# Moving four sub-key score products and two weight steps into the last projection, with a branch hint, in an attention and PEER block

## The chip, the cores and the metric

The kernel runs on one core of a Trainium2 chip. A core has a matmul engine (TensorE, PE in the profile, its weight loads shown apart as PEld), a vector engine (VectorE, DVE), an engine for activations and copies (ScalarE, ACT), a general one (GpSimd, POOL), and an engine that mainly issues transfers (SyncE, SP). They run their own instruction streams and meet at semaphores. The metric is the device time of one execution in microseconds; lower is better. The kernel before takes 1779.33 us, the median of three runs (1779.2 to 1783.94).

## The reference, cut to what matters

One sequence of N = 2048 rows of D = 448 features goes through two blocks, both with a layer norm in front and a residual sum behind. The first is attention with 16 heads of 28 features. The second is PEER: each row picks, per head, 8 of 4096 experts by two lists of 64 sub-keys, and sums their outputs.

```python
q  = jnp.einsum("nd,dhc->nhc", xf, w_q)            # 16 heads, 2 x 256
s1 = jnp.einsum("nhd,ed->nhe", q[..., :dk], k1)    # 64 sub-key scores
s2 = jnp.einsum("nhd,ed->nhe", q[..., dk:], k2)    # 64 sub-key scores
# the 8 best of s1, of s2, and of their 64 sums, per head
g   = softmax(top_s)                               # over the 8 chosen experts
act = gelu(einsum("nd,nhkd->nhk", xf, u[top_e]))
out = einsum("nhk,nhk,nhkd->nd", g, act, v[top_e])
```

All is float32. The kernel writes a product as a high part times a high part plus two corrections, so that a product over 448 features is 11 matmuls (`products`).

## The kernel before, in words

The rows are worked on in four blocks of 512 (`b` = 0 to 3), each of four tiles of 128 (`j` = 0 to 3). The kernel has these stages.

1. `qkv` (up to about 158 us): layer norm, queries, keys and values for all rows, stored to device memory. It also computes a bound on the attention scores and writes a flag for whether it is exceeded; then the last values are made, each copied by ACT and stored to `v_d` by a transfer from ACT's queue (lines 355 and 356).
2. The branch on the flag (`values_load` on line 422, `tc.If` on line 423). It is taken by PE, DVE and SP. The body, which fixes up queries for large scores, isn't executed with these inputs. On the path around it SyncE steps through eight semaphores that the body would have raised.
3. Attention (about 158 to 940 us) for 16 units of (block, four heads). Woven into it are the folding of the sub-keys into the query weights (`Fold`; results in `wp_d`, four tensors of four heads each), the split of the expert weights, and, for blocks 0 to 2, the projection behind attention (`project`) and the search for the best sub-keys (`search`).
4. The last projection, of block 3, and then the sub-key scores of block 3 (about 940 to 1046 us), with the first block's expert weights beside them. This is where the change is.
5. The experts, block after block (about 1046 us to the end): scores of all rows with all 4096 experts, `gelu`, multiplication with the dense matrix `G` of weights, and the product with `v`.

In stage 4 three generators are woven.

- `project(3, 2, room)`, 12 steps and a closing one. Each of the four tiles passes six steps: transposes of the attention output on PE and a copy on ACT; the low parts on DVE (`lows`, lines 109 and 110); the product with `wo` on PE, 11 matmuls, and a copy on ACT (line 567); residual sum, statistics on DVE (lines 569, 603, 604), and the reciprocal root on POOL (lines 96 and 97); the norm on DVE (line 100), transposes on PE and a copy on ACT (line 577); the low parts on DVE. A tile starts two steps after the one before. The closing step has SyncE store the result to `x_d` (lines 589 and 590).
- `weights(0, G)`, called `w0`, 34 steps: one loads `st`, one makes the first factors, and then 32 steps of 16 rows. Each has DVE prepare the next 16 rows (line 835, a comparison `p`, and in turn line 814, `f`, or line 820, `fg`), PE do 32 small matmuls (line 850), and ACT copy the result to `G` (line 852). Two buffers hold `p` and two PSUM banks the results (name `A`).
- `kept_scores(3, pools)`, called `sc`, 20 steps. The 16 heads are four groups (`g`) of four. For each group one step has SyncE load the folded keys, a high and a low half of 1 MB each (line 627), and four steps, one for each tile, have PE do 11 matmuls (line 80, `M<-w,XHb` and `M<-w,XLb`) and ACT copy the result to a `ring` buffer (line 630). The groups use two buffers in turn: `sw0` for groups 0 and 2, `sw1` for groups 1 and 3. `sw1` lies where the projection's buffers were, so that it is opened after `r2.close()`.

`scores_of` and all of the projection's products and transposes take their PSUM result tile under the name `M`, of which there are two.

The order of the work on each engine is the order in which the program issues it (`manual_schedule`); nothing is reordered. It comes from `weave`: each generator has a number of steps and a stretch from `lo` to `hi`, its steps are put at equal distances in the stretch, and the earliest goes next. So a pair of numbers such as 0.05, 0.27 sets which step of one generator stands in front of which step of another, on every engine on which both issue something, SyncE's queue among them.

Between the two calls of `weave` in stage 4 three loads of expert weights are issued (`load_u`, line 934); after the second, the rows of block 0 are loaded (`load_X`).

Of the kernel before, what the change touches and what calls it, by code (L numbers as in the profile page):

```python
# [18 lines left out]
ET = mybir.EngineType  # L19
# [36 lines left out]
def block(ctx: ExitStack, tc: tile.TileContext, x, wqk, wv, wo, wq, k12, uT, v, cst, out):  # L56
# [57 lines left out]
    def weave(*gens):  # L114


        gens = [[lo + 0.5 * (hi - lo) / n, (hi - lo) / n, g] for g, n, lo, hi in gens]
        while gens:
            e = min(gens, key=lambda e: e[0])
            e[0] += e[1]  # L120
            if next(e[2], end) is end:
                gens.remove(e)
# [144 lines left out]
    with ExitStack() as c0:  # L267
# [81 lines left out]
        def values_of(b):  # L349
            for j in range(4):  # L350
                c = slice(128 * j, 128 * j + 128)
                pv = ps.tile([128, D], F32, name="pq", bufs=4)
                mm_all(pv, products(lambda t: XH[b][:, t, c], lambda t: XL[b][:, t, c],
                                    lambda t: wvh[:, t], lambda t: wvl[:, t]))
                nc.scalar.activation(vst[j][:, :, :DH], pv.rearrange("p (h d) -> p h d", h=H), AF.Copy)
                (nc.scalar if b > 1 else nc.sync).dma_start(v_d[:, b, :, j].rearrange("g p c -> p g c"),
                                                                    vst[j].rearrange("p (g h) d -> p g (h d)", g=4))
# [3 lines left out]
        def qkv():  # L361
            for b in range(NB):
                normed(b)
                if b < 2:
                    values_of(b)
            load_wqk(0)
            for g in range(4):
                w = wqks.pop(g)
                if g < 3:
                    load_wqk(g + 1)  # L370
                kmax = wk.tile([128, 8], F32, name="kmax")
                for b in range(NB):
                    pk = proj(w[0], b)
                    sq = wk.tile([128, 512], FR, name="sq")
                    nc.scalar.activation(sq, pk, AF.Square, scale=SCALE)
                    kf = wk.tile([128, 512], F32, name="f", tag="f")
                    nc.scalar.activation(kf, pk, AF.Identity, bias=ct[:, C_ONE:C_ONE + 1], scale=SCALE)
                    store(ks_d[g], b, kf)
                    pn = ps.tile([128, 512], F32, name="tr")
                    nc.tensor.matmul(pn, blk, sq, start=True, stop=True)  # L380
                    nc.vector.reduce_max(kmax[:, b:b + 1], pn, axis=AX.X)
                nc.vector.reduce_max(kmax[:, 4:5], kmax[:, :4], axis=AX.X)
                nc.vector.tensor_scalar(kmax[:, 4:5], kmax[:, 4:5], 1.002, None, op0=OP.mult)
                for b in range(NB):
                    pq = proj(w[1], b)
                    sq = wk.tile([128, 512], FR, name="sq")
                    nc.scalar.activation(sq, pq, AF.Square)
                    pn = ps.tile([128, 512], F32, name="tr")
                    nc.tensor.matmul(pn, blk, sq, start=True, stop=True)
                    bd = wk.tile([128, 512], F32, name="bd", bufs=1)  # L390
                    nc.scalar.activation(bd, pn, AF.Sqrt, scale=kmax[:, 4:5])
                    nc.vector.reduce_max(kmax[:, b:b + 1], pn, axis=AX.X)
                    qf = wk.tile([128, 512], F32, name="f", tag="f")
                    nc.vector.scalar_tensor_tensor(qf, bd, ct[:, C_NEG:C_NEG + 1], pq, op0=OP.mult, op1=OP.add)
                    store(qs_d[g], b, qf)
                nc.vector.reduce_max(kmax[:, 5:6], kmax[:, :4], axis=AX.X)
                nc.vector.tensor_tensor(big[:, g:g + 1], kmax[:, 4:5], kmax[:, 5:6], op=OP.mult)
                if g == 1:
                    load_q(0)
                    for n in range(2):  # L400
                        load_kv(n)
                if g == 2:
                    fold.append(Fold(raw_p))
            bigm = wk.tile([128, 1], F32, name="bigm")
            nc.vector.reduce_max(bigm, big, axis=AX.X)
            nc.vector.tensor_scalar(bigm, bigm, BOUND * BOUND, None, op0=OP.is_gt)
            warm = wk.tile([128, 1], F32, name="warm")
            nc.scalar.activation(warm, bigm, AF.Exp)
            pf = ps.tile([1, 128], F32, name="tr")
            nc.tensor.transpose(pf, bigm, ident)  # L410
            bm = wk.tile([1, 1], F32, name="bm")
            nc.vector.reduce_max(bm, pf, axis=AX.X)
            nc.vector.tensor_copy(flag, bm)
            for b in range(2, NB):
                values_of(b)

        qkv()

    att = ExitStack()
    P = {0: att.enter_context(tc.tile_pool(name="pm", bufs=1, space=PSUM, reuse_waits="tile"))}  # L420

    isbig = nc.values_load(flag[0:1, 0:1], engines=(ET.PE, ET.DVE, ET.SP), min_val=0, max_val=1)
    with tc.If(isbig != 0):  # L423
        with ExitStack() as c1:
            gp = c1.enter_context(tc.tile_pool(name="lpg", bufs=1))
            pg = c1.enter_context(tc.tile_pool(name="psg", bufs=1, space=PSUM))
            kS = gp.tile([128, N], FR, name="kSg")
            qS = gp.tile([128, N], FR, name="qSg")
            mx = gp.tile([128, NT], F32, name="mx")
            old = gp.tile([NT, 2, 128], F32, name="old")  # L430
            new = gp.tile([NT, 2, 128], FR, name="new")
            for h in range(H):
                g, j = divmod(h, 4)
                r = slice(32 * j, 32 * j + 32)
                for i in range(4):
                    p = slice(32 * i, 32 * i + 32)
                    nc.sync.dma_start(kS[p].bitcast(F32), ks_d[g][K_ROWS[i], r])
                    nc.sync.dma_start(qS[p].bitcast(F32), qs_d[g][Q_ROWS[i], r])
                for i in range(2):
                    nc.sync.dma_start(old[:, i], qs_d[g][i, 32 * j + 28].rearrange("(a b) -> a b", a=NT))  # L440
                for t in range(NT):
                    S = pg.tile([128, N], F32, name="Sg")
                    for c in range(4):
                        nc.tensor.matmul(S[:, 512 * c:512 * c + 512], qS[:, 128 * t:128 * t + 128],
                                         kS[:, 512 * c:512 * c + 512], start=True, stop=True)
                    nc.vector.reduce_max(mx[:, t:t + 1], S, axis=AX.X)
                mt = P[0].tile([NT, 128], F32, name="M")
                nc.tensor.transpose(mt, mx, ident)
                nc.vector.tensor_tensor(old[:, 0], old[:, 0], old[:, 1], op=OP.add)
                nc.vector.tensor_tensor(old[:, 0], old[:, 0], mt, op=OP.subtract)  # L450
                nc.vector.tensor_copy(new[:, 0], old[:, 0])
                nc.vector.tensor_tensor(new[:, 1], old[:, 0], new[:, 0].bitcast(F32), op=OP.subtract)
                for i in range(2):
                    nc.sync.dma_start(qs_d[g][i, 32 * j + 28].rearrange("(a b) -> a b", a=NT), new[:, i].bitcast(F32))
            halves(qs[0], qs_d[0], slice(0, 512))
# [399 lines left out]
    WEIGHTS = 34  # L855
# [81 lines left out]
    with tc.manual_schedule(engines={ET.PE, ET.DVE, ET.Activation, ET.Pool, ET.SP}):  # L937
        room = {"xt": [ring[4 * j + 2] for j in range(4)], "at": [ring[3], ring[7]]}
        pools = [tc.tile_pool(name="sw0", bufs=1, side="right", reuse_waits="tile")]
        with ExitStack() as c1:  # L940
            pools = [c1.enter_context(pools[0])]
            w0, sc = weights(0, G), kept_scores(3, pools)
            weave((project(3, 2, room), 12, 0, 0.25), (islice(w0, 1), 1, 0.01, 0.02), (islice(sc, 1), 1, 0.02, 0.03),
                  (islice(w0, 6), 6, 0.05, 0.27))
            r2.close()
            be = ctx.enter_context(tc.tile_pool(name="be", bufs=3, reuse_waits="tile"))
            for f in range(3):
                us[f] = load_u(f)
            c2 = c1.enter_context(ExitStack())
            pools.append(c2.enter_context(tc.tile_pool(name="sw1", bufs=1, reuse_waits="tile")))  # L950
            weave((w0, WEIGHTS - 7, 0.27, 1), (sc, 19, 0.27, 0.88))
            load_X(0)
    bv = ctx.enter_context(tc.tile_pool(name="bv", bufs=3, reuse_waits="tile"))
    gw = ctx.enter_context(tc.tile_pool(name="gw", bufs=2, side="right", reuse_waits="tile"))
# [128 lines left out]
```

## Time and profile before

| | |
|---|---|
| median of three runs | 1779.33 us |
| the profiled execution | 1780.06 us |
| its span, first to last instruction | 1778.3 us |
| mean granted clock of TensorE | 0.987 |
| busy time of PE, DVE, ACT, POOL | 1705.5, 1137.3, 885.1, 396.7 us |

The page of the profile gives the busy time of each engine and the span in 40 slices; with it go groups of instructions by line, the waits (who waited for whom), the chain of work that ended last, and the timeline, in which one row stands for one instruction or for several of a kind that follow each other (x11). Times in the timeline are the start in us from the span's start and the duration in us; in square brackets stands the idle time of that engine before it and what ended it. A table by stage gives the busy time of every engine within a stretch, the granted clock (1.00 is full speed) and the busy share of the DMA engines.

### The profile page before, as it was taken

Reading aid. Unit: us, or ns where it says so; the run is one execution under the profiler, and the core shown is the slowest. Engines: PE = TensorE matmul, PEld = TensorE weight load, DVE = VectorE, ACT = ScalarE, POOL = GpSimd, SP = SyncE. Lnnn points to the kernel's source line nnn. Section 1 sums busy time; section 2 is a strip of 40 time slices with the busy share of each in tenths; the row PEclk is TensorE's granted clock in tenths of the full one; section 3 lists DMA queues with packets and bytes.
Section 4 is the critical chain, followed back from the end, with each engine's and each line's share of the span. In section 5 each row is a group of like instructions: output and inputs, shape, how many; then the busy total and the mean of one; then the engine's idle time right before and its main releaser. Section 6 shows DMA issues by size and latency. Waiting matters only on the chain.

```text
span 1778.3 us, 36155 instructions
## 1 busy us (share of the span) xinstructions
PE 1705.5 (96%) x14113; PEld 1164.2 (65%) x14113; DVE 1137.3 (64%) x3584; ACT 885.1 (50%) x1176; POOL 396.7 (22%) x450
## 2 busy tenths in 40 slices
PE   7998999999999899989996999999999999999999
PEld 6775434445544445444544888888888888888888
DVE  6653665444777548764776789526994599249722
ACT  3544767876677666866683342223422243224321
POOL 3451455321176224662271000000000000000000
PEclk9998999999999999999998999999999999999999
DMA  8754788568865787478841545766466745674564
GB/s 255 251 185 141 257 268 260 181 219 301 312 210 170 285 311 257 154 257 336 298 140 63 199 153 190 230 220 208 129 196 194 238 143 178 195 254 153 166 199 156
DMA packets 141744, 378.41 MB, mean 213 GB/s; under 512 B 13568, under 2 KB 40960, under 8 KB 133376
## 3 DMA queue, kind: packets, MB, share of 16 engines
q1 hardware_dynamic: 137344, 373.94, 63.1%
q8 instruction: 114, 1.87, 0.4%
q10 hardware_dynamic: 4224, 2.10, 0.4%
q14 instruction: 62, 0.51, 0.1%
HBM read 298.39 MB, written 77.59 MB: 211 GB/s over the span
## 4 chain that ended last, share of the span: by engine, by line
PE 73%; DVE 9%; POOL 2%; issue 1%; ACT 1%; DMA 0%; DVEq 0%; POOLq 0%
PE M L80 20%; PE acc L1006 16%; PE A L501 10%; PE S L476 10%; PE A L80 8%; PE A L850 5%; DVE ti L676 1%; DVE pos L703 1%; DVE ti L675 1%; ACT P L479 1%; PE M L106 1%; DVE p L835 0%; POOL sel L727 0%; PE M L489 0%; DVE ts L702 0%
## 5 line engine op out<-in xcount | busy, mean ns | idle before, releaser
L479 ACT ACTIVATE P<-S 128x1024 f32<-128x1024 f32 x512 | 495.9, 1023 | 89.2 <-PE S L476 87.7
L1006 PE MATMUL acc<-v,w 128*128 128x448 f32 x1536 | 329.7, 369 | 0.4 <-DMA v<-vs 0.2
L1006 PEld LDWEIGHTS acc<-v,w 128*128 128x128 f32 x1536 | 288.0, 188 | 33.2 <-ACT w L980 1.0
L501 PE MATMUL A<-P,V 128*32 128x512 f32 x2048 | 279.4, 614 | 0.0
L476 PE MATMUL S<-qS,kS 32*128 32x512 f32 x3072 | 272.2, 433 | 5.7 <-SPq L423 5.0
L476 PEld LDWEIGHTS S<-qS,kS 32*128 32x128 f32 x3072 | 145.2, 186 | 160.6 <-issue 99.2
L980 ACT ACTIVATE w<-ring 128x512 fp32r<-128x512 f32 x128 | 80.6, 632 | 223.9 <-PE acc L1006 161.5
L835 DVE TENSOR_TENSOR p<-st,iota 128x2048 f16<-128x2048 f16 x128 | 154.6, 1220 | 37.2 <-PE A L850 35.5
L981 DVE TENSOR_TENSOR w<-ring,w 128x512 fp32r<-128x512 f32 x128 | 87.3, 688 | 120.2 <-ACT w L980 120.0
L80 PE MATMUL A<-XHb,u 128*128 128x512 f32 x568 | 143.6, 394 | 0.0
L80 PE MATMUL M<-w,XHb 128*128 128x512 f32 x512 | 137.9, 412 | 5.1 <-ACT st L84 5.0
L675 DVE MAX8 ti<-fresh 128x8 f32<-128x64 f32 x384 | 80.6, 210 | 85.1 <-ACT fresh L657 85.1
L979 DVE TENSOR_TENSOR ring<-ring,G 128x512 f32<-128x512 f32 x128 | 85.5, 684 | 74.1 <-ACT ring L966 70.5
L80 PEld LDWEIGHTS M<-w,XHb 128*128 128x128 f32 x512 | 92.4, 190 | 61.3 <-issue 31.1
L850 PEld LDWEIGHTS <-p 128*128 128x128 f16 x4096 | 108.7, 97 | 25.3 <-issue 14.5
L850 PE MATMUL A<-fg,p 128*128 128x32 f16 x4096 | 116.7, 177 | 5.0 <-DVE p L835 4.9
L80 PE MATMUL M<-XHb,u 128*128 128x512 f32 x456 | 120.3, 403 | 0.0
L80 PEld LDWEIGHTS A<-XHb,u 128*128 128x128 f32 x568 | 106.0, 188 | 21.6 <-ACT ring L966 0.7
L966 ACT ACTIVATE ring<-M 128x512 f32<-128x512 f32 x57 | 34.2, 600 | 142.6 <-PE M L80 142.6
L501 PEld LDWEIGHTS A<-P,V 128*32 128x32 f32 x2048 | 41.8, 108 | 93.9 <-issue 86.8
L966 ACT ACTIVATE ring<-A 128x512 f32<-128x512 f32 x71 | 42.3, 596 | 103.8 <-PE A L80 103.8
L852 ACT ACTIVATE G<-A 128x512 f32<-128x512 f32 x128 | 76.7, 599 | 34.3 <-PE A L850 34.0
(178 smaller groups left out, 2298.7 us busy)
## 6 DMA issues: line engine op xcount, KB each, us to landing
u<-us SPq DMA_DIRECT2D x128, 512.0 KB, 3.6
w<-wp SPq DMA_DIRECT2D x56, 1024.0 KB, 7.9
v<-vs SPq DMA_DIRECT2D x128, 448.0 KB, 3.3
kS<-ks SPq DMA_DIRECT2D x64, 512.0 KB, 4.8
V<-vd SPq DMA_DIRECT2D x64, 256.0 KB, 3.0
us<-hl SPq DMA_DIRECT2D x32, 512.0 KB, 6.3
wr<-in_wq_dram SPq DMA_DIRECT2D x32, 448.0 KB, 5.7
vs<-hl SPq DMA_DIRECT2D x32, 448.0 KB, 5.7
```

Of the source, the lines that this page charges most:

```text
L80: nc.tensor.matmul(ps, l, r, start=i == 0, stop=i == len(pairs) - 1)
L476: nc.tensor.matmul(S[j // 2][:, j % 2], kS[r, a, 128 * (k % 4):128 * (k % 4) + 128], qS[r, c], start=m == 0, stop=m == 2)
L479: nc.scalar.activation(Pt[:, 2 * i:2 * i + 2], S[i], AF.Exp)
L501: nc.tensor.matmul(O[n][32 * j:32 * j + 32], V[:, k % 4, j], Pt[:, j], start=k == 0, stop=k == NT - 1)
L675: nc.vector.max(t8[:, 4 * i + k], src[:, 64 * k:64 * k + 64])
L835: newest[0] = nc.vector.tensor_tensor(p1, pairs(0, s, TG, 128), ids(TG, 128), op=OP.is_equal).ins
L850: nc.tensor.matmul(ps[:, t], p1[:, a, :, u], f[:, s % TF // 2 + a, k, :, u], start=k == 0, stop=k == 1)
L852: nc.scalar.activation(G[:, :, s:s + TG], ps.rearrange("p t f -> p f t"), AF.Copy, scale=1.0 / GS)
L979: nc.vector.tensor_tensor(a, a, G[:, f], op=OP.mult)
L980: nc.scalar.activation(w[:, 0], a, AF.Copy)
L981: nc.vector.tensor_tensor(w[:, 1], a, w[:, 0].bitcast(F32), op=OP.subtract)
L1006: nc.tensor.matmul(acc[j][:, :D], l, r, start=f == 0 and k == 0, stop=f == 31 and k == 2)
```

## The change

It has two parts.

In the first weave of stage 4, `w0` makes 8 steps in place of 6, and `sc` makes four steps in the stretch from 0.125 to 0.29: the four products of group 0. In the second weave `w0` has two steps less, `sc` four less, and the stretches begin at 0.29 in place of 0.27; that of `sc` ends at 0.92 in place of 0.88. By the numbers the order after the change is as follows (P is a step of the projection, W one of the weights that multiplies, S a score, each counted from 0): P0 P1 P2 P3 W0 P4 P5 W1 P6 S0 W2 P7 W3 P8 S1 P9 W4 P10 S2 W5 P11 W6, the closing step, S3; then the three loads, W7, the load of group 1, W8, and the first score of group 1. Before it was P0 to P4, W0, P5, P6, W1, P7, P8, W2, P9, W3, P10, P11, W4, the closing step; then the three loads, W5, S0, W6, S1, W7, S2, W8, S3, W9, the load of group 1, W10, W11 and the first score of group 1.

At the branch, the `If` gets a label, and right after the flag is written a hint for that branch is put into the streams of PE, DVE and SP. A hint asks for the instructions at the branch's target to be fetched ahead. The values of blocks 2 and 3 are issued between the hint and the branch.

```diff
             nc.vector.reduce_max(bm, pf, axis=AX.X)
             nc.vector.tensor_copy(flag, bm)
+            tc.mark_branch_hint_location("bound", engines=(ET.PE, ET.DVE, ET.SP))
             for b in range(2, NB):
                 values_of(b)
...
     isbig = nc.values_load(flag[0:1, 0:1], engines=(ET.PE, ET.DVE, ET.SP), min_val=0, max_val=1)
-    with tc.If(isbig != 0):
+    with tc.If(isbig != 0, label="bound"):
...
             weave((project(3, 2, room), 12, 0, 0.25), (islice(w0, 1), 1, 0.01, 0.02), (islice(sc, 1), 1, 0.02, 0.03),
-                  (islice(w0, 6), 6, 0.05, 0.27))
+                  (islice(w0, 8), 8, 0.05, 0.27), (islice(sc, 4), 4, 0.125, 0.29))
             r2.close()
...
-            weave((w0, WEIGHTS - 7, 0.27, 1), (sc, 19, 0.27, 0.88))
+            weave((w0, WEIGHTS - 9, 0.29, 1), (sc, 15, 0.29, 0.92))
             load_X(0)
```

## The prediction

> **What bounds the kernel now.** I read the page first.
>
> ```profile
> span 1778.3 us, 36155 instructions
> ...
> PE 1705.5 (96%) x14113; PEld 1164.2 (65%) x14113; DVE 1137.3 (64%) x3584; ACT 885.1 (50%) x1176; POOL 396.7 (22%) x450
> ...
> PEclk9998999999999999999998999999999999999999
> ```
>
> TensorE is busy for 96% of the span, so a gain can only come from its idle time or from its clock. Two places matter: the branch on the flag near 158 us, and the last projection with what follows it, which begins near 942 us. The busy time by stage, cut at 975.1 us (the last projection is complete) and at 992.1 us, is:
>
> ```profile
> 942.00:975.10 33.10, 21.77 (x234) 18.58 (x234) 25.75 (x44) 9.81 (x17) 2.98 (x8) 0.84 0.16 50
> 975.10:992.10 17.00, 15.11 (x170) 12.27 (x171) 12.98 (x13) 4.18 (x7) 0.00 (x0) 0.80 0.84 325
> 992.10:1046.00 53.90, 51.62 (x876) 42.92 (x875) 42.54 (x41) 20.96 (x35) 0.00 (x0) 1.00 0.33 121
> ```
>
> The columns are length, then busy time of PE, PEld, DVE, ACT and POOL, granted clock, DMA share and GB/s. TensorE is idle for 33.10 - 21.77 = 11.3 us in the projection, 1.9 us in the next 17 us, and 2.3 us from there to 1046. The 11.3 us are what the new work is put into. Here is why they exist: the last row tile's own chain, in order of time.
>
> ```profile
> 962.19 0.29 DVE L110 TENSOR_TENSOR oh<-M,oh 64x128 fp32r<-64x128 f32 x1
> ...
> 963.44 1.06 PE L80 MATMUL M<-woh,oh 128*128 128x448 f32 x4
> ...
> 965.15 0.78 PE L80 MATMUL M<-woh,ol 128*128 128x448 f32 x3
> ...
> 965.96 0.54 ACT L567 ACTIVATE ring<-M 128x448 f32<-128x448 f32 x1 [1.73 <-PE M L80]
> ...
> 967.12 0.62 DVE L569 TENSOR_TENSOR ring<-ring,ring 128x448 f32<-128x448 f32 x1
> ...
> 968.44 0.18 DVE L604 BATCH_NORM_AGGREGATE mv<-st 128x2 f32<-128x6 f32 x1
> ...
> 968.97 0.55 POOL L97 TENSOR_TENSOR rstd<-rstd,lnpow 128x1 f32<-128x1 f32 x1
> ...
> 969.52 1.22 DVE L820 TENSOR_TENSOR fg<-f,st 128x2048 f16<-128x2048 f16 x1
> 970.67 1.22 DVE L835 TENSOR_TENSOR p<-st,iota 128x2048 f16<-128x2048 f16 x1
> 971.80 0.51 DVE L100 TENSOR_SCALAR xn<-ring,mv,rstd 128x448 f32<-128x448 f32 x1
> 972.46 1.09 PE L106 MATMUL M<-ct,xn 128*128 128x128 f32 x4 [4.23 <-DVE xn L100]
> ...
> 974.21 0.56 DVE L109 TENSOR_TENSOR XLb<-M,XHb 128x384 fp32r<-128x384 f32 x1 [1.90 <-ACT XHb L577]
> 974.78 0.29 DVE L110 TENSOR_TENSOR XHb<-M,XHb 64x128 fp32r<-64x128 f32 x1
> 975.11 0.69 DVE L814 TENSOR_TENSOR f<-st,iota 128x1024 f16<-128x1024 f16 x1
> 975.72 1.22 DVE L835 TENSOR_TENSOR p<-st,iota 128x2048 f16<-128x2048 f16 x1
> ```
>
> It alternates between five engines. A step of weights on VectorE stands inside it already: the two instructions from 969.52 to 971.80 take 2.28 us, and TensorE waits 4.23 us for what is queued behind them. The other kind of step, L814 and a compare, takes 0.61 us to its second start and so about 1.75 us in all. When the chain ends, at 975.07, SyncE proceeds:
>
> ```profile
> 975.14 0.32 SPq L589 DMA_DIRECT2D xd<-XHb  x1
> 975.51 0.42 SPq L590 DMA_DIRECT2D xd<-XLb  x1
> 976.02 3.51 SPq L934 DMA_DIRECT2D u<-us  x3
> 979.64 1.16 SPq L627 DMA_DIRECT2D w<-wp  x2
> ...
> DMA to landing us min/median/max: 10.0/10.8/11.7
> ```
>
> The last line is the time to landing of the two transfers of 979.64, which bring the folded keys of the second four heads (group 1). Their first half lands at 979.64 + 10.0 = 989.6, their second at about 980.3 + 11.7 = 992.0: 14.5 and 16.9 us after the projection is complete, for they queue behind two stores and three loads. TensorE then looks like this:
>
> ```profile
> 983.09 2.11 PE L80 MATMUL M<-w,XHb 128*128 128x512 f32 x8
> ...
> 985.75 0.97 PE L850 MATMUL A<-fg,p 128*128 128x32 f16 x32
> 986.57 2.12 PE L80 MATMUL M<-w,XHb 128*128 128x512 f32 x8
> ...
> 995.80 2.09 PE L80 MATMUL M<-w,XHb 128*128 128x512 f32 x8
> ```
>
> From start to start a score product (11 matmuls) costs 985.75 - 983.09 = 2.66 us and a step of weights (32) costs 986.57 - 985.75 = 0.82. Group 1 is first used at 995.80. So the four products of group 0 are what hides those transfers today, with 3.8 us to spare.
>
> **The change part by part.** *Scores into the projection.* Four products of group 0, 4 x 2.66 = 10.6 us of TensorE, move ahead, three of them into the idle time and the fourth just behind the projection. Two weight steps, 1.6 us of TensorE and 1.75 + 2.28 = 4.0 us of VectorE, move with them, and the step times in the weave now put a step of compares in front of each norm and in front of the last lows, where before only the last norm had one. ACT's four evacuations move too, each about the 0.54 us of the L567 row, hidden beside the products. No DMA moves in program order: the stores, the three loads and the keys of group 1 still come in that order, behind the projection's end.
>
> The chain again, with the new work in its place. The third tile's product before it ran at half clock:
>
> ```profile
> 957.90:961.30 3.40, 3.40 (x11) 2.76 (x9) 2.26 (x2) 0.60 (x1) 0.00 (x0) 0.50 0.06 16
> ```
>
> With a weight step ahead of it I take it at full clock, which gives back 3.4/2 = 1.7 us; a compare step of 1.75 more ahead of the last tile's first lows takes them again, and these end at 962.5 as before. The first score then occupies TensorE to 965.3, two weight steps to 966.9, the last tile's product (963.44 to 965.93 in the rows, 2.4) to 969.3, the copy to 969.9, sum and statistics (967.12 to 968.62, 1.5) to 971.4, POOL with its hand-over (0.9) to 972.3. A compare step of 1.75 goes first, then the norm: 974.6. The transposes and their copy take about 1.5, but VectorE has a 2.28 us step to 976.8 ahead of the lows of 0.86. The projection is complete at 977.7 in place of 975.07: **+2.6 us**. The second score fits into the old 4.23 us wait. Bounds of this term: 0 if idle time takes all, and +9.4 by the second rival below.
>
> *The wait that follows.* After 977.7 TensorE has the third score's tail, the weight steps, the fourth score and two steps more: about 6.2 us, to 984. Then comes the first product of group 1, whose keys land 14.5 and 16.9 us after 977.7, at 992.2 and 994.6. What is queued behind it on TensorE is every further step, and VectorE can only fill the two compare buffers. So about **8 us of idle time come back**, which takes most of what the projection gave. From 994.6: 7/11 of a product (1.7), 11 products (29.3), 23 steps at 0.81 (18.6), the 2.3 us of compare waits in the third stage row, and the clock:
>
> ```profile
> 158.10:166.00 7.90, 7.18 (x48) 3.21 (x52) 5.66 (x5) 3.88 (x4) 2.35 (x1) 0.50 0.60 185
> ...
> 977.80:981.80 4.00, 4.00 (x18) 3.18 (x15) 4.00 (x5) 0.60 (x1) 0.00 (x0) 0.50 1.00 315
> ```
>
> After two other pauses the granted clock was 0.50 for 4.0 and for 7.9 us of work; 2.4 us of that pass before the second half lands, which leaves (1.6 to 5.5)/2 = 0.8 to 2.7 us lost. I take 1.5. The end: 994.6 + 1.7 + 29.3 + 18.6 + 2.3 + 1.5 = 1048.0, against 1046.0: **+2.0 us**. From there on TensorE is the bound and the shift passes on.
>
> The Trainium skill, "TensorE: Matmul & The Clock Gate", section "What's actually happening", says that one idle window of about 3.4 us halves the clock and one busy window restores it; that speaks against a pause of 8 us, and the rows agree on the halving, while 7.9 us is longer than its one window. An estimate by that page would be 1.7 us in place of 1.5, and the end 0.2 us later.
>
> *The hint.* The branch on the flag, with the page's fetches between 155.2 and 156.6:
>
> ```profile
> L423 SPq EVENT_SEMAPHORE  x8: 17/17/17, 151.6 to 158.0; - x8
> ...
> L423 PEldq COMPARE_BRANCH  x1: 4368/4368/4368, 150.0 to 150.0; - x1
> ...
> 153.78 0.37 ACTq L356 DMA_DIRECT2D vd<-vst  x1
> ...
> 158.14 2.07 PE L476 MATMUL S<-qS,kS 32*128 32x512 f32 x14 [4.97 <-SPq L423]
> ...
> DMA to landing us min/median/max: 3.9/3.9/3.9
> ...
> q8 instruction: 1, 0.02, 5.1%
> ```
>
> TensorE's branch takes 4.37 us from 150.0, over at 154.4, yet its first matmul waits for SyncE's eight semaphore steps, which end at 158.0. They follow the landing of the last store of V, issued at 153.78 and landed 3.9 us later. So the branch's own time is hidden; what shows is that landing. I put 1.6 of its 3.9 us down to the one instruction fetch that falls into it,
>
> ```profile
> DMA to landing us min/median/max: 2.3/2.3/2.3
> ```
>
> which is what the store two before it took to land. If the hint moves that fetch forward, 1.6 us go. The other end is no gain, and a cost of three short instructions, which no row shows; by the 17 ns of a semaphore step they are nothing. I take **-1.6 us**, as the only fetch in that stretch is one that follows the branch.
>
> Sum: +2.0 - 1.6 = +0.4. The profiled execution took 1780.06 us, 0.73 above the median of 1779.33; by it the sum gives 1780.5, by the median 1779.7. I forecast **1780.0 us**: no change that a measurement of this kernel could tell, which is about 0.3%, or 5.3 us.
>
> **The rivals.** *The keys come in time.* If both halves of group 1 landed within 6.2 us of the projection's end, the 8 us wait would be gone: 983.9 + 12 x 2.66 + 23 x 0.81 + 2.3 = 1036.7, 9.3 us early, and with the hint 1768.4 us. For it speaks only that SyncE is idle in the projection; against it the rows of SyncE, in program order behind the stores. Half of the way there, and the hint, give 1774.
>
> *The last tile's chain pays for all of it (slower).* If only the 4.23 us wait covers the three scores (8.0), two steps (1.6) and the compares (4.0), the projection ends 13.6 - 4.2 = 9.4 us later, not 2.6. Everything behind shifts by 6.8 more: 1779.3 + 2.0 + 6.8 = 1788.1 us, and 1786.5 with the hint. It decides from a delay of 2.6 + 5.3 - 2.0 = 5.9 us on, or 7.5 with the hint's gain. For it: two PSUM buffers named M serve both the chain and the scores, so a score must wait for a buffer and then holds it.
>
> *The hint frees TensorE alone.* By this rival the branch is what holds TensorE, and it starts at about 154.5, 3.6 us early: 1777.7 us with the +2.0. Against it: the wait in the row of 158.14 names SyncE. The Trainium skill, "Runtime: NRT & Kernel Launch", section "Instruction fetch mechanics", states that a taken branch out of the loaded window stalls for a fetch; the 4368 ns branch agrees, but the rule alone does not say who waits. If the hint does nothing at all, the time is 1781.3.
>
> **How the numbers follow.** My forecast with the hint's two ends has 0.52, the keys in time, wholly or half, 0.18, the paying chain 0.22, TensorE freed by the hint 0.08. Faster by over 0.3% (below 1774.0) is the first rival, 0.18; slower (above 1784.7) is the second, 0.22; the rest, 0.60, is within. The range takes in half of the first rival and most of the second: 1771 to 1786.5. The likeliest case alone holds 1777 to 1783.
>
> **What would show it.** After the change: products L80 M<-w,XHb between 955 and 980; a wait of 7 to 9 us on TensorE, released by the DMA w<-wp, shortly after the three loads of u; a granted clock of 0.5 behind it; the projection's last L110 near 978; the last weight step near 1048. At the branch: the 4368 ns gone, and the first matmul of S near 156.5. I am wrong if there is no wait for w<-wp, if the projection ends after 981, or if compares on VectorE hold TensorE for more than 4 us behind the wait.

## The result, and the profile after

The changed kernel takes 1782.5 us, the median of fourteen runs (1777.78 to 1787.77); the kernel before, beside it, 1780.71 us (1778.56 to 1784.11). The ratio is 1.0008, with a 95% interval of 0.9998 to 1.0018: no change that can be measured. The profiled execution took 1777.78 us, the shortest of the fourteen and 4.7 us below their median, so single stretches are compared here, not its span.

The page of the changed kernel:

```profile
span 1776.0 us, 36157 instructions
PE 1700.6 (96%) x14113; PEld 1159.9 (65%) x14113; DVE 1134.5 (64%) x3584; ACT 884.8 (50%) x1176; POOL 397.4 (22%) x450
PEclk9999999999999999999999899999999999999999
```

TensorE is still the bound at 96%. Its last projection begins at 937.52 and is complete at 972.80; the first half of the second four heads' keys is there at 986.96; the experts begin at 1042.0. Busy time by stage, with the columns length, PE, PEld, DVE, ACT, POOL, granted clock, DMA share and GB/s:

```profile
155.90:157.80 1.90, 1.20 (x14) 0.74 (x14) 1.79 (x3) 0.90 (x1) 0.00 (x0) 0.99 0.28 100
157.80:161.20 3.40, 3.23 (x18) 1.03 (x18) 3.37 (x3) 2.92 (x4) 2.34 (x1) 0.50 0.73 232
...
937.52:972.80 35.28, 27.25 (x267) 22.49 (x267) 29.75 (x47) 10.98 (x19) 4.21 (x8) 0.95 0.15 46
972.80:986.96 14.16, 6.05 (x140) 5.25 (x140) 8.89 (x9) 3.59 (x6) 0.00 (x0) 0.77 0.95 370
986.96:990.64 3.68, 3.32 (x7) 2.22 (x8) 0.00 (x0) 0.00 (x0) 0.00 (x0) 0.50 1.01 427
990.64:1042.00 51.36, 49.59 (x867) 41.40 (x866) 42.84 (x43) 20.52 (x35) 0.00 (x0) 1.00 0.23 88
```

The idle time has moved. The projection takes 35.28 us, against 32.84 before (942.24, the first transposes, to 975.08), and TensorE idles for 35.28 - 27.25 = 8.0 us in it, 11.3 before. Behind it TensorE idled for 1.9 of 17 us before; now it is busy for only 6.05 of the first 14.16, while the DMA engines are 95% busy. Its own rows, in order of time, name the transfer:

```profile
974.43 2.11 PE L80 MATMUL M<-w,XHb 128*128 128x512 f32 x8
...
977.08 1.77 PE L851 MATMUL A<-fg,p 128*128 128x32 f16 x64
986.96 2.08 PE L80 MATMUL M<-w,XHb 128*128 128x512 f32 x4 [8.11 <-DMA w<-wp]
989.40 1.75 PE L80 MATMUL M<-w,XHb 128*128 128x512 f32 x4 [0.36 <-DMA w<-wp]
```

TensorE finishes the fourth product and two steps of weights, then waits 8.11 us, and 0.36 for the second half. SyncE's queue shows why the keys are late; it is the same order as before, and starts the moment the projection is complete (the x4 in the last row are the two halves of group 1 and, behind them, those of group 2):

```profile
972.86 0.32 SPq L590 DMA_DIRECT2D xd<-XHb  x1
973.23 0.42 SPq L591 DMA_DIRECT2D xd<-XLb  x1
973.75 3.54 SPq L935 DMA_DIRECT2D u<-us  x3
977.40 3.36 SPq L628 DMA_DIRECT2D w<-wp  x4
```

At the branch, first the instructions on its line (count, duration in ns, first and last start in us), then the timeline:

```profile
L424 SPq EVENT_SEMAPHORE  x8: 17/17/17, 151.1 to 155.8; - x8
L424 PEldq COMPARE_BRANCH  x1: 388/388/388, 149.5 to 149.5; - x1
```

```profile
153.24 0.37 ACTq L356 DMA_DIRECT2D vd<-vst  x1
...
155.90 1.20 PE L477 MATMUL S<-qS,kS 32*128 32x512 f32 x14 [3.27 <-SPq L424]
```

TensorE's branch takes 388 ns for 4368 before, and the first matmul of S starts 155.90 - 153.24 = 2.66 us after the last store of V is issued, for 4.36 before. TensorE is still released by SyncE.

A correction to the description of the change above: the hints do not run where they are written, behind the flag. In the trace's instruction records they stand at the head of the three engines' streams, at 0.72 to 0.80 us, 50 to 51 ns each.

### The profile page after: what moved, and what is told of

The parts are those of the page before. It is cut to its first block, busy times and chain, and to the rows that moved or that the text cites. A ratio compares the mean times of both kernels' runs of the same rounds, so it can differ in the third digit from the quotient of the medians.

```text
span 1776.0 us, 36157 instructions
## 1 busy us (share of the span) xinstructions
PE 1700.6 (96%) x14113; PEld 1159.9 (65%) x14113; DVE 1134.5 (64%) x3584; ACT 884.8 (50%) x1176; POOL 397.4 (22%) x450
## 4 chain that ended last, share of the span: by engine, by line
PE 72%; DVE 8%; DMA 2%; POOL 2%; issue 1%; ACT 1%; SPq 0%; DVEq 0%; POOLq 0%; ACTq 0%
PE M L80 20%; PE acc L1007 16%; PE A L502 10%; PE S L477 10%; PE A L80 9%; PE A L851 5%; DVE ti L677 1%; DVE pos L704 1%; DMA w<-wp 1%; DVE ti L676 1%; ACT P L480 1%; PE M L106 0%; POOL sel L728 0%; DVE ts L703 0%; PE M L490 0%
```

## The experiments

My theory: the scores do fill the projection, but they were the cover of the keys of group 1, so that 8 us come back as a wait, plus some 2.5 us of a longer projection; and the hint is worth what the last store of V gains when one instruction fetch leaves its way. The rivals are those of the prediction.

### The hint alone, and the weave alone

```diff
 (the hint alone: the kernel before, and)
+            tc.mark_branch_hint_location("bound", engines=(ET.PE, ET.DVE, ET.SP))
-    with tc.If(isbig != 0):
+    with tc.If(isbig != 0, label="bound"):
```

The weave alone is the changed kernel without these lines.

> The hint and the label alone, the weave as before. Theory (the branch's own fetch is hidden, but a fetch behind it delays the last store of V): TensorE's branch falls from 4.37 us to below 0.5, the last store of V lands 2.3 us after its issue in place of 3.9, the first matmul of S follows it by 2.7 us in place of 4.4, and the whole is 1.6 to 2.3 us shorter than before (ratio 0.9987 to 0.9991); the projection and what follows it look as before. Rival, the hint frees TensorE alone: 3.6 us or more. Rival, it does nothing: ratio 1.000 and the store still lands after 3.9 us.

> The two calls of weave as after, without hint and label. Theory (most of the gain in the projection is given back as a wait for the keys of group 1): from the first transposes of the projection to the first product of the experts 104 to 106 us, where it was 103.8 before; a wait of about 8 us released by the DMA w<-wp; the branch as before (4.37 us); in all 0.5 to 2.5 us longer than before, ratio 1.0003 to 1.0014. Rival, the last tile's chain pays for all: the projection's last lows end 7 us or more later against its start, ratio above 1.003. Rival, the scores are hidden and nothing takes their place: 8 us shorter, ratio 0.9955.

The kernel before, beside these and the next two, took 1780.52 us. The hint alone: 1779.1 us, ratio 0.9984 (0.9973 to 0.9994), so 2.8 us less (1.1 to 4.8). The weave alone: 1783.29 us, ratio 1.0014 (1.0005 to 1.0023), so 2.5 us more (0.9 to 4.1). They add up to -0.3 us, just within the interval of the whole change, -0.4 to +3.2; its median, +1.8, is 2.1 us above their sum. With the hint alone the first matmul of S started 155.38 - 152.72 = 2.66 us behind the store; with the weave alone 159.23 - 154.68 = 4.55. The stages of the weave alone, as in the table above:

```profile
943.61:978.92 35.31, 27.31 (x267) 22.50 (x267) 29.74 (x47) 10.99 (x19) 4.20 (x8) 0.95 0.15 46
978.92:993.39 14.47, 6.07 (x140) 5.26 (x139) 8.89 (x10) 3.60 (x6) 0.00 (x0) 0.76 0.96 371
993.39:1000.20 6.81, 6.45 (x55) 4.56 (x56) 0.10 (x1) 0.70 (x2) 0.00 (x0) 0.51 0.78 330
```

Projection and wait are those of the changed kernel within 0.4 us (35.31 and 14.47, for 35.28 and 14.16). What differs is the half clock behind the wait: 6.81 us of it for 3.68, and half of the difference, 1.6 us, is about what this kernel is later by the experts' start: 1049.50 - 943.61 = 105.89 us from the projection's first transposes, for 1042.0 - 937.52 = 104.48. So the moved scores cost time, and the hint gains some: two effects of opposite sign, not two of no effect. That they cancel exactly isn't shown.

### What delays the keys

The first kernel issues the keys of group 1 ahead of the three loads of u; the second also puts the projection's two stores behind them, so that the keys no longer wait for the projection's end in SyncE's queue. Both are the changed kernel otherwise.

```diff
 (both)
-            for f in range(3):
-                us[f] = load_u(f)
             c2 = c1.enter_context(ExitStack())
             pools.append(c2.enter_context(tc.tile_pool(name="sw1", ...)))
-            weave((w0, WEIGHTS - 9, 0.29, 1), (sc, 15, 0.29, 0.92))
+            next(sc)
+            keep_X(3)                  # the second kernel only
+            for f in range(3):
+                us[f] = load_u(f)
+            weave((w0, WEIGHTS - 9, 0.29, 1), (sc, 14, 0.332, 0.92))
 (the second, at the end of project; keep_X holds the two stores)
-        nc.sync.dma_start(x_d[b][:, :4], XH.bitcast(F32))
-        nc.sync.dma_start(x_d[b][:, 4:], XL.bitcast(F32))
+        if not room:
+            keep_X(b)
```

> As after, but the transfers of the keys of group 1 are issued ahead of the three loads of u (1.5 MB), still behind the two stores. Theory (TensorE waits for bytes that queue in front of the keys): at some 310 GB/s the three loads are 4.8 us, so the wait of 8.1 us falls to about 3.3, the stage ends 4 to 5 us earlier than after, ratio to before about 0.9975. Rival (the wait is set by compares on VectorE, or by the time to bring 2 MB alone): wait and time stay as after.

> As the run with the keys first, but the two stores of the projection's result stand behind the keys as well, so nothing is in front of them. Theory: 1.75 MB less in front, 5 us more; the keys land some 6 to 7 us after the projection's end, when TensorE has just done its last free work, so the wait is 0 to 1 us and the half clock behind it is gone; the stage ends 8 to 10 us earlier than after, ratio to before about 0.995 to 0.996. Rival (the second stage is bound by VectorE's compares once the wait is gone): waits for p take the place of the wait for w, and no more than half of that is won.

Keys ahead of the loads: 1777.45 us, ratio to before 0.9985 (0.9976 to 0.9994). Keys ahead of loads and stores: 1769.26 us, ratio 0.9937 (0.9924 to 0.995), which is faster than both kernels. SyncE's queue and TensorE's product in the timeline of the first of them:

```profile
975.99 0.32 SPq L590 DMA_DIRECT2D xd<-XHb  x1
...
976.89 2.19 SPq L628 DMA_DIRECT2D w<-wp  x2
979.13 2.61 SPq L935 DMA_DIRECT2D u<-us  x3
```

```profile
986.21 2.08 PE L80 MATMUL M<-w,XHb 128*128 128x512 f32 x4 [4.24 <-DMA w<-wp]
```

and in the second:

```profile
973.62 0.79 SPq L633 DMA_DIRECT2D w<-wp  x2
976.00 0.32 SPq L595 DMA_DIRECT2D xd<-XHb  x1
...
976.86 1.46 SPq L940 DMA_DIRECT2D u<-us  x3
```

```profile
980.21 1.77 PE L856 MATMUL A<-fg,p 128*128 128x32 f16 x64
981.83 2.07 PE L80 MATMUL M<-w,XHb 128*128 128x512 f32 x8
```

with the second kernel's table by stage for the 10 us behind its projection:

```profile
975.93:986.00 10.07, 10.07 (x214) 8.76 (x214) 9.47 (x11) 4.77 (x8) 0.00 (x0) 1.00 0.99 372
```

The wait goes from 8.11 to 4.24 to nothing: in the second kernel the product at 981.83, the first of group 1, follows the weight steps with no gap, and the table has TensorE busy for all of 10.07 us at full clock. The DMA engines are as busy (0.99, 372 GB/s) as they were under the wait (0.95, 370), but now with bytes that nobody waits for. From the projection's first transposes to the experts it takes 96.32 us (938.66 to 1034.98), for 104.5 in the changed kernel and 103.8 before (942.24 to 1046.01); and that although its projection takes 37.27 us, 2.0 more than the changed kernel's, with a granted clock of 0.50 from 960.13 to 963.55.

The second step from 4.24 us to nothing has two parts. The keys are issued 975.93 - 973.62 = 2.31 us ahead of the projection's end, in the first kernel 976.89 - 975.92 = 0.97 us behind it; and with nothing in front of them they land 6.7 us after their issue (median), for 10.0 in the first. The first kernel fell short of what was expected: 4.24 us of wait, not 3.3, and from the first transposes to the experts 100.89 us, 3.6 less than the changed kernel, not 4 to 5. The second gained the 8.2 us expected there, and by whole runs a little more than expected. The prediction's rival that the keys come in time was priced at 1768.4 us; here, where they are made to, it is 1769.26.

### The order without the moved scores

Is the order of issue simply better by itself? This kernel has the hint, the weave of before, and the order of the best one; the keys of group 1 are issued by a function of their own, and `kept_scores` takes them from there.

```diff
 (the kernel before with the hint, and)
+            early[1] = keys(1, pools)
+            keep_X(3)
             for f in range(3):
                 us[f] = load_u(f)
...
-            w = pools[g % 2].tile(...)  # and its two loads
+            w = early.pop(g) if g in early else keys(g, pools)
```

> The hint and the weave of before, with the order of issue of the best run: the folded keys of group 1 first, then the two stores of the last projection's output, then the three loads of u. Theory (the order pays only because the moved scores leave a wait of 8 us for those keys): with the four products of group 0 still behind the projection there is no wait to take away, and the time is that of the hint alone, 1779 us, ratio to before 0.998; from the first transposes of the projection to the first expert product 102 to 103.5 us (102.77 with the hint alone). Rival (the order is a gain by itself, the moved scores add little): ratio near 0.994, and those two starts about 96 us apart.

It took 1778.63 us, ratio 0.999 (0.9978 to 1.0003), to 1780.67 before; the two stages of it (projection, then up to the experts) are:

```profile
939.02:971.85 32.83, 21.74 (x234) 18.53 (x234) 25.57 (x43) 9.80 (x17) 2.98 (x8) 0.84 0.18 54
971.85:1042.77 70.92, 66.72 (x1045) 55.20 (x1045) 55.55 (x55) 25.18 (x42) 0.00 (x0) 0.95 0.45 168
```

That is 103.75 us, as before (103.77), a little above the stretch expected; the two stages before are 32.84 and 70.93. So the order alone is worth nothing that shows, and the moved scores alone cost; only together do they gain. Each removes the limit that hides the other.

### The scores without the two steps of weights

```diff
-                  (islice(w0, 8), 8, 0.05, 0.27), (islice(sc, 4), 4, 0.125, 0.29))
+                  (islice(w0, 6), 6, 0.05, 0.27), (islice(sc, 4), 4, 0.125, 0.29))
-            weave((w0, WEIGHTS - 9, 0.29, 1), (sc, 15, 0.29, 0.92))
+            weave((w0, WEIGHTS - 7, 0.29, 1), (sc, 15, 0.29, 0.92))
```

> The changed kernel without the two more steps of weights: six steps and four scores within the projection. My account of the projection's lengthening (2.4 us) puts it down to steps of compares on VectorE, 1.75 and 2.28 us each, that come in front of the last tile's norm and lows; so without two of them the projection is back to 32 to 33.5 us, the wait for the keys of group 1 stays at 8 us behind it, and with 1.6 us of weight steps more behind the wait the two starts (first transposes, first expert product) lie 103 to 104 us apart (104.47 with the whole change): ratio to before about 0.9995. Rival (the scores themselves, in TensorE's queue ahead of the chain's products, lengthen it): the projection stays at 35 us and the two starts lie 105.5 to 106.5 us apart, ratio 1.001.

It took 1779.48 us, ratio 0.9995 (0.9985 to 1.0004). That interval does not part it from the changed kernel; the stages do:

```profile
940.61:974.83 34.22, 26.89 (x232) 22.64 (x233) 25.65 (x43) 10.40 (x18) 2.97 (x8) 0.90 0.15 48
974.83:988.89 14.06, 6.11 (x112) 4.96 (x110) 8.80 (x10) 2.99 (x5) 0.00 (x0) 0.80 0.95 369
988.89:1046.10 57.21, 54.94 (x936) 45.57 (x937) 46.96 (x48) 21.93 (x37) 0.00 (x0) 0.96 0.27 108
```

My expectation missed in the stages. Without the two steps the projection is 34.22 us, only 1.06 below the changed kernel, not 2 to 3; and the two starts are 105.49 us apart, at the rival's end. The profiled execution, 1782.26 us, is the slowest of the ten, though, 2.8 us above their median; by the whole runs the ratio is the 0.9995 expected, and the interval leaves the rival's 1.001 out.

The rows say more than the sums. The last tile's product starts 964.32 - 940.61 = 23.71 us after the first transposes, for 24.37 in the changed kernel and 21.20 before. So most of its delay is there without the two steps: the first score stands in TensorE's order ahead of this product. And the 1.06 us is what two effects leave. With the two steps the third tile's product runs at full clock (1.00 from 952.25 to 954.72); without them it falls into a clock of 0.50 (955.94 to 959.36), as in the kernel before. That takes away most of what two steps less on VectorE would have given.

Behind the wait the two steps take 57.21 - 55.04 = 2.2 us away: 1.6 that they are themselves on TensorE, and some 0.5 by a shorter half clock (3.68 us of it, for 4.60 without them). Whether they earn their place in the projection, the whole runs don't show.

### Whose branch the hint is for

Two kernels with the weave of before, one with the hint on TensorE alone, one with it on VectorE and SyncE alone:

```diff
+            tc.mark_branch_hint_location("bound", engines=(ET.PE,))
 (and)
+            tc.mark_branch_hint_location("bound", engines=(ET.DVE, ET.SP))
```

> The weave of before, and the hint on TensorE alone. In the run with the hint on all three engines the first matmul of S started 2.66 us after the issue of the last store of V (4.36 before), and TensorE's branch took 383 ns (4368 before). Theory (the one instruction fetch that lies on the store's way is the one that TensorE's own branch orders): the same two numbers as with all three, 2.7 us and about 0.4 us. Rival (the fetch is ordered by SyncE or VectorE): the branch of TensorE is short, but the first matmul stays near 4.4 us behind the store.

> The weave of before, and the hint on VectorE and SyncE alone. Theory (the fetch is TensorE's): TensorE's branch stays near 4 us and the first matmul of S near 4.4 us behind the issue of the last store of V. Rival (the fetch is SyncE's or VectorE's): 2.7 us, with TensorE's branch still at 4 us beside it.

They took 1778.73 and 1780.36 us, one run each, which says little; their rows say more. With the hint on TensorE alone, its branch and the timeline:

```profile
L424 PEldq COMPARE_BRANCH  x1: 383/383/383, 149.0 to 149.0; - x1
```

```profile
152.77 0.37 ACTq L356 DMA_DIRECT2D vd<-vst  x1
155.41 1.20 PE L477 MATMUL S<-qS,kS 32*128 32x512 f32 x14 [3.26 <-SPq L424]
```

With the hint on the other two, its branch, the timeline, and of the transfers between 153 and 159 us the queue of instruction fetches and the store's time to landing:

```profile
L424 PEldq COMPARE_BRANCH  x1: 3902/3902/3902, 149.5 to 149.5; - x1
```

```profile
153.28 0.37 ACTq L356 DMA_DIRECT2D vd<-vst  x1
157.92 2.08 PE L477 MATMUL S<-qS,kS 32*128 32x512 f32 x14 [5.25 <-SPq L424]
```

```profile
q8 instruction: 1, 0.02, 1.8%
...
vd<-vst ACTq DMA_DIRECT2D x1, 256.0 KB, 4.1
```

and the same store in the changed kernel, whose transfers between 153 and 159 us show no fetch:

```profile
vd<-vst ACTq DMA_DIRECT2D x1, 256.0 KB, 2.2
```

2.64 us from store to matmul with TensorE's hint, 4.64 without it, with SyncE's and VectorE's hints in place; the store lands 4.1 us after its issue without TensorE's hint and 2.2 after it with the hint on all three; with the hint on TensorE alone no fetch stands in that stretch either. So the fetch goes with TensorE's own branch, and it is SyncE's wait for ACT's store that pays for it. The other kernels agree: the seven with a hint on TensorE have 2.64 to 2.67 us from store to matmul, the three without it 4.36 to 4.64.

The fetch comes behind the branch, not within it. In the kernel before, the branch is over at 154.4 us and the fetch begins at 155.4; no other transfer's packet starts from 155.65 to 156.5, and then the store's last nine follow. With the hint on the other two engines the branch is over at 153.4 and the fetch begins at 154.1. In the changed kernel the branch is over at 149.9 and the only fetch near it begins at 150.6, 2.6 us before the store is issued. The kernel before has one more there, at 151.0 within the branch, and one more on that queue in the whole run (114 for 113). So it isn't shown whether the fetch behind the branch moves ahead or falls away with the hint; either way it is off the store's way.

## Why the prediction was right, and where it was not

The sum was +0.4 us and the forecast 1780.0; measured is 1782.5 against 1780.7, so +1.8 by the medians (the interval of the ratio holds -0.4 to +3.2). Term by term:

**The projection's end** (+2.6 us). The chain was written out step by step, and the trace follows it. The rows of the last row tile, after the change:

```profile
957.63 2.11 PE L80 MATMUL M<-w,XHb 128*128 128x512 f32 x8 [1.62 <-issue]
...
961.89 1.05 PE L80 MATMUL M<-woh,oh 128*128 128x448 f32 x4
...
964.39 0.54 ACT L568 ACTIVATE ring<-M 128x448 f32<-128x448 f32 x1 [1.72 <-PE M L80]
...
966.82 0.55 POOL L97 TENSOR_TENSOR rstd<-rstd,lnpow 128x1 f32<-128x1 f32 x1
...
967.99 1.22 DVE L836 TENSOR_TENSOR p<-st,iota 128x2048 f16<-128x2048 f16 x1
969.12 0.51 DVE L100 TENSOR_SCALAR xn<-ring,mv,rstd 128x448 f32<-128x448 f32 x1
...
972.50 0.29 DVE L110 TENSOR_TENSOR XHb<-M,XHb 64x128 fp32r<-64x128 f32 x1
```

Counted from the projection's first transposes (942.24 before, 937.52 now), the prediction and the trace have: the last tile's product starts at 24.7 and 24.4 us, its copy is done at 27.7 and 27.4, POOL at 30.1 and 29.9, the norm at 32.4 and 32.1, the last lows at 35.5 and 35.3. The compare step ahead of the norm (967.99) and the one ahead of the last lows are where they were expected. So is the full clock of the third tile's product (1.00 from 952.25 to 954.72), which the prediction took to give back 1.7 us. It was only afterwards that I put the lengthening down to the compares alone, which the run without the two weight steps showed to be wrong.

**The wait** (about 8 us). The halves of the keys were to land 14.5 and 16.9 us after the projection is complete; TensorE takes them up 14.16 and 16.60 us after it, and waits 8.11 and 0.36. Putting the keys ahead of the other bytes, and then ahead of the projection's end as well, takes the wait away in two steps. That settles the mechanism.

**Behind the wait** (1.5 us of half clock, in a stretch of 1048.0 - 994.6 = 53.4 us). It took 1041.99 - 989.40 = 52.6 us. The half clock lasted for 3.68 us of the work in the changed kernel, 1.8 us lost counted from the first half, and 6.81 with the weave alone, 3.4 us lost. The prediction counts from the second half's landing: by that 1.24 us of half clock are left in the changed kernel (989.40 to 990.64), 0.6 us lost, and 4.38 with the weave alone (995.82 to 1000.20), 2.2 lost. So of its 0.8 to 2.7 us the low end was too high, and 1.5 was about 0.9 too much for the changed kernel; nearly the same stop of TensorE gave the one and the other. One of its two rows was read wrongly, too: the half clock of 977.80 to 981.80 began at 971.53, ahead of the last pause before it (2.59 us, up to 976.99). The Trainium skill, "TensorE: Matmul & The Clock Gate", section "What's actually happening", has one busy window of some 3.4 us restore the clock, and says that the windows run freely, whenever the work begins. By that, an estimate from the page, the first whole window ends between 3.4 and 6.8 us after the work starts again; 3.68 and 6.81 us are near its two ends, and my estimate by one window alone left half of the rule out. The 3.99 and 4.60 us of two other kernels (keys ahead of the loads, and without the two weight steps) lie between them. The 7.9 us of the prediction's own row at the start of attention, in which TensorE is busy for 7.18, are above both ends, so what restores the clock is not settled here.

**The stage as a whole** (+2.0 us). From first transposes to the experts it is 104.5 us and, with the weave alone, 105.89, against 103.8: +0.7 and +2.1. With the hint alone, where the weave is that of before, it is 102.77 us, so one profile can be off by 1 us and the +0.7 by itself says nothing. The times of whole runs with the weave alone say +2.5 (0.9 to 4.1).

**The hint** (-1.6 us). From store to matmul it gave -1.70, by the fetch named; the whole runs say -2.8 (1.1 to 4.8 less), which holds it. What I had not priced is the half clock at the start of attention: before it covers the 7.9 us from 158.10 to 166.00 of the prediction's row, in the changed kernel the 3.40 us of the second row of its table. What that is worth is not settled. From the first matmul of S to the projection the changed kernel took 937.52 - 155.90 = 781.62 us and the kernel before 942.24 - 158.14 = 784.10; but the changed kernel's profile is the shortest of its runs, and the other seven kernels with a hint lie on both sides of the kernel before, at 783.44 to 785.09.

**The rivals.** That the last tile's chain pays for all is refuted by the chain's rows; that the hint frees TensorE alone, by the wait for SyncE that still stands in the rows of the changed kernel and of both with a part of the hint. That the keys come in time did not happen, for the reason given against it, and its price was right to 0.9 us once an experiment made it happen. That it came so close is luck in part: the stage gained 103.77 - 96.32 = 7.5 us there, where the rival has 9.3. None of the conditions for being wrong came about: the wait for the keys is there, the projection is complete at 972.80 (35.28 us long, where 981 would be 38.8), and VectorE's compares hold TensorE behind the wait for 1.5 us in four times, the longest 0.5:

```profile
PE M L80 <- DMA w<-wp: 8.5, 2, 8.1
PE M L106 <- DVE xn L100: 2.9, 2, 1.8
...
PE A L851 <- DVE p L836: 1.5, 4, 0.5
```

(waits of TensorE between 940 and 1047 us in the changed kernel: total, times, longest). Of the second line 1.15 us, at the last tile, is what is left of the 4.23 us wait that the scores were put into; the other 1.75 lies at the first tile's norm, which had no such wait before.

## What to carry to other kernels

Before work is moved forward into idle time, ask what it covers where it stands: here four products hid the landing of the next group's keys, and with them gone TensorE stood still for 8.1 us behind the projection until the keys were there. Move the issue of what is needed next along with the work, ahead of transfers that nobody waits for: the same move then gained 0.6% (with the hint, which alone is 0.16%), while the order alone gained nothing that shows. And a change that comes out at nothing may be two effects that cancel; run its parts alone.

## What the runs showed that I had not expected

- A hint that runs at 0.8 us shortens a branch at 149 us, from 3902 to 4368 ns to 383 to 388, and without it on TensorE the landing of ScalarE's store takes 4.1 us in place of 2.2. The Trainium skill, "Runtime: NRT & Kernel Launch", section "Instruction fetch mechanics", has the stall of a taken branch for its fetch, which agrees; the cost here was the store's.
- The clock can fall after the work has begun again. In the changed kernel TensorE starts attention at 155.90 us after a pause, with the granted clock at 0.99 for the next 1.9 us, and only then has 3.40 us at 0.50, in which it is busy for 3.23.
- In all eight kernels with a hint of any kind the last store of V was issued at 152.56 to 153.28 us, for 153.78 before and 154.68 with the weave alone, though the work ahead of it is the same. None of the runs settles why.
